# LN, FFN and the output projection of a decode layer: VectorE block transposes in place of selector matmuls, contiguous weight reads, and one load of wo summed in row layout

## The chip, the cores and the metric

The kernel runs on one core of one Trainium2 chip. The metric is device time in microseconds (us), median of several executions. Spans in the traces are shorter than the times (184.9 against 186.1 us in one and the same execution). Each program is traced in one of its executions only, and the stream of loads can lie some tenths of a microsecond earlier or later from one trace to the next (the matmuls that wait for w_up start at 177.45 us in the kernel before, at 177.06 in after_warm); so compare distances within a trace before absolute times. Ratios are computed as the mean time of one kernel's fast runs over that of the other's fast runs of the same rounds, so they are not quite the ratio of the medians quoted beside them.

The engines: PE is TensorE (PEld its weight loads), DVE is VectorE, ACT is ScalarE, POOL is GpSimd, SP issues the DMAs. The granted TensorE clock was not full all the time: "0.50" below is half of full speed, as from 41.79 to 45.20 us in the trace of the kernel before.

## The reference, cut to what matters

One token for each of two batch rows goes through an adaLN-conditioned layer: attention over the last 1024 positions of a cache, then a GEGLU FFN. D = 640, 32 heads of 192, F = 1536, all bf16.

```python
mod = silu(c) @ w_mod                     # six vectors of 640: sa, ca, ga, sb, cb, gb
h = layernorm(x) * (1 + ca) + sa
q = (h @ wq)                              # 640 -> 6144, 32 heads
o = softmax(q k^T / sqrt(192)) v          # for each head, 1024 cached positions
x = x + ga * (o @ wo)                     # 6144 -> 640
h = layernorm(x) * (1 + cb) + sb
x = x + gb * ((gelu(h @ w_gate) * (h @ w_up)) @ w_down)   # 640 -> 1536 -> 640
```

With one token, every weight and cache element is used once or twice: the work is to read 76.88 MB.

## The kernel before

The program has one instruction list for each engine, ordered by semaphores. One SP queue issues all big loads in a fixed order into one arena in SBUF: w_mod, wq, the K and V tiles, wo, w_gate, w_up, w_down. A load waits until the tile whose place it takes has been consumed. The vectors live in "row layout": 640 numbers as 4 groups of 160, group i of batch row b on partition 32*i + 16*b. The kernel's matmuls take them along the partitions instead (h2T in the trace: 128 partitions x 10), so it turns each hidden vector. These are the parts that matter (cut):

```python
WO_SPLIT = [(0, 39), (39, 9)]             # wo in two loads
...
# LN output -> matmul operand: 20 small matmuls with a selector, then a cast out of PSUM
for j in range(KT):
    for i in range(NR):
        e.matmul(ps[32*i:32*i+32, BK_M, CT+2*j:CT+2*j+2], lhsT=hv[:, :, j], rhs=selrow[:, i, :], ...)
S.op("dve", lambda e: e.tensor_copy(out=dst_bf, in_=ps[:, BK_M, CT:CT+2*KT]...))
...
# wo: 4 column groups of TensorE each take every fourth k-tile; two halves of 320 columns
for tl in range(n):
    i = t % NR
    for bk, lo, w in ((2, 0, NA), (3, NA, NA)):
        e.matmul(ps[32*i:32*i+B, bk, 0:w], lhsT=oT[:, t, :], rhs=wv[:, tl, lo:lo+w], ...)
# ... evacuated by ACT and DVE, then summed into row layout by 4 f32 matmuls with selw
...
# gate and up: group i takes columns m*12 + i*3 + r of the weights: runs of 3, 12 apart
wk = wv[:, k, :].rearrange("p (m i r) -> p i m r", i=NR, r=FR)
e.matmul(ps[32*i:32*i+B, bk, 0:FT]..., lhsT=h2T[:, k, :], rhs=wk[:, i, :, :], ...)
...
# FFN activation -> operand of down: 3 matmuls with a selector, then a cast
# down: three loads of w_down (8, 3 and 1 of 12 rows), 48 matmuls of 17 x 160
```

`keep_clock(n)` issues n matmuls on unused data whose only purpose is to keep TensorE busy, so that its clock is not lowered: with 10 of them between gate and up, 8 between up and down and 13 ahead of wo (split_warm below), up ran at a granted clock of 1.00 instead of 0.50 (after_split2).

Of the kernel before, what the change touches and what calls it, by code (L numbers as in the profile page):

```python
# [5 lines left out]
ALU = mybir.AluOpType  # L6
# [113 lines left out]
def bass_adaLN_cond__sliding_block_cached__geglu_ffn__decode_kernel(  # L120
# [29 lines left out]
    FR = 3  # L150
    FC = F // P
    assert B == 2 and D == KT * P and XQ * J == W and XQ * H == P and HB * NR == H and NT * P == NQ
    assert DD * NT == Dh and DD * H == P and NR * FR == FC and FC * P == F and DR == KT * 32 and DD == XQ
# [17 lines left out]
    WO_SPLIT = [(0, 39), (39, 9)]  # L171
# [13 lines left out]
    with es:  # L185
# [18 lines left out]
        place[("wo", 1)] = (13 * HS, wo_n[1])  # L204
        assert 4 * HS + wo_n[0] <= 9 * HS and wo_n[1] <= HS
# [27 lines left out]
        selrow = sb("selrow", [P, NR, B], BF16)  # L233
# [18 lines left out]
        hT = sb("hT", [P, KT, B], BF16)  # L252
        h2T = sb("h2T", [P, KT, B], BF16)
# [7 lines left out]
        oT = sb("oT", [P, NT, B], BF16)  # L261
        selw = sb("selw", [P, RM], F32)
        gl = sb("gl", [P, FT], F32)
        aR = sb("aR", [P, FT], BF16)
        selg = sb("selg", [P, NR, B], BF16)
        aT = sb("aT", [P, FC, RM], BF16)
# [11 lines left out]
        def bank(k):  # L278
            return ("bank", k)
# [67 lines left out]
        for nm, t in (("scT", scT), ("aT", aT)):  # L347
            S.op("pool", lambda e, t=t: e.memset(t[:, :, :], 0.0), writes=[nm], name=nm + "0")
# [8 lines left out]
        S.op("pool", lambda e: e.affine_select(out=selrow[:, :, :], in_=ones_b[:, 0:1].unsqueeze(2).broadcast_to([P, NR, B]),  # L357
                                                pattern=[[-32, NR], [-RB, B]],
                                                compare_op=ALU.is_equal, fill=0.0, base=0, channel_multiplier=1),
             reads=["ones_b"], writes=["selrow"], name="selrow")  # L360
        S.op("pool", lambda e: e.affine_select(out=selg[:, :, :], in_=ones_b[:, 0:1].unsqueeze(2).broadcast_to([P, NR, B]),
                                                pattern=[[-32, NR], [-1, B]],
                                                compare_op=ALU.is_equal, fill=0.0, base=0, channel_multiplier=1),
             reads=["ones_b"], writes=["selg"], name="selg")
        S.op("pool", lambda e: e.memset(selw[:, :], 0.0), writes=["selw"], name="selw0")
        for i in range(NR):
            S.op("pool", lambda e, i=i: e.affine_select(out=selw[:, 0:RM:RB], in_=selw[:, 0:RM:RB], pattern=[[-1, B]],
                                                        compare_op=ALU.not_equal, fill=1.0, base=-32 * i, channel_multiplier=1),
                 reads=["selw"], writes=["selw"], name="selw%d" % (i + 1))
# [66 lines left out]
        def ln_mod(tag, opc_idx, s_idx, dst_bf):  # L436
# [9 lines left out]
            def f(e):  # L446
                last = None
                hv = hrow[:, :].rearrange("p (m j) -> p m j", j=KT)
                for j in range(KT):
                    for i in range(NR):  # L450
                        last = e.matmul(ps[32 * i:32 * i + 32, BK_M, CT + 2 * j:CT + 2 * j + 2], lhsT=hv[:, :, j], rhs=selrow[:, i, :],
                                        start=(j == 0), stop=(j == KT - 1), skip_group_check=True, tile_position=(0, 32 * i))
                return last
            S.op("pe", f, reads=["hrow", "selrow"], writes=[bank(BK_M)], name=tag + "_T")
            S.op("dve", lambda e: e.tensor_copy(out=dst_bf[:, :, :], in_=ps[:, BK_M, CT:CT + 2 * KT].rearrange("p (j b) -> p j b", b=B)),
                 reads=[bank(BK_M)], writes=[tag + "_out"], name=tag + "_out")
# [27 lines left out]
        for w, (k0, nk) in enumerate(WQ_SPLIT):  # L484
            def f(e, w=w, k0=k0, nk=nk):
                last = None
                wv = view(("wq", w)).rearrange("p (k i n) -> p k i n", k=nk, i=NR)
                for kk in range(nk):
                    k = k0 + kk
                    for n in range(NQB):  # L490
                        for i in range(NR):
                            last = e.matmul(ps[32 * i:32 * i + B, n, :], lhsT=hT[:, k, :], rhs=wv[:, kk, i, n * QW:(n + 1) * QW],  # L492
                                            start=(k == 0), stop=(k == KT - 1), tile_position=(0, 32 * i))
# [124 lines left out]
        def p_sel(e):  # L618
            last = None
            for dd in range(DD):  # L620
# [6 lines left out]
        keep_clock(9, "clock0")  # L627

        S.op("act", lambda e: e.activation(out=oT[:, :, :].rearrange("p t b -> p b t"),
                                           in_=ps[:, BK_OT, 0:B * NT].rearrange("p (b t) -> p b t", b=B), func=ACTF.Copy),  # L630
             reads=[bank(BK_OT)], writes=["oT"], name="oT")
        S.op("act", lambda e: e.activation(out=junk[:, :], in_=epsc[:, 0:1], func=ACTF.Sqrt), reads=["epsc"], writes=["junk"], name="sqrt_table")
        S.op("dve", lambda e: e.memset(ps[:, 0:4, :], 0.0), writes=[bank(z) for z in range(4)], name="init_W")
        NA = D // 2
        for ci, (t0, n) in enumerate(WO_SPLIT):
            def f(e, ci=ci, t0=t0, n=n):
                last = None
                wv = view(("wo", ci)).rearrange("p (t n) -> p t n", t=n)
                for tl in range(n):
                    t = t0 + tl  # L640
                    i = t % NR
                    for bk, lo, w in ((2, 0, NA), (3, NA, NA)):
                        last = e.matmul(ps[32 * i:32 * i + B, bk, 0:w], lhsT=oT[:, t, :], rhs=wv[:, tl, lo:lo + w],  # L643
                                        start=(t < NR), stop=(t >= NT - NR), tile_position=(0, 32 * i))
                return last
# [129 lines left out]
```

## Time and profile before

| | before |
|---|---|
| time, median of 3 (range) | 186.01 us (185.92 to 186.16) |
| span of the profiled run | 184.9 us |
| bytes read, mean rate | 76.88 MB, 416 GB/s |
| busy share of the load queue | 96.9% |
| last landing (third part of w_down) | about 182.0 us |

The first lines to read are the page's. The slices cut the span into 40 equal parts; "DMA" is the mean busy share of the 16 DMA engines in tenths, "GB/s" what they moved, and the third line gives a queue's packets, MB and share of the span:

```profile
DMA  9999998999897999999898989899999989899980
GB/s 349 433 495 425 425 425 362 429 425 495 367 511 340 511 404 447 457 394 479 374 479 365 500 351 500 383 468 436 425 450 394 491 367 486 378 388 435 419 365 28
...
q1 hardware_dynamic: 2604, 76.88, 96.9%
```

There is no slice in which the loads stop before the last one. The cause of the alternation of 340 and 511 GB/s was not looked for.

The second view is the timeline of the tail, from the arrival of wo. Columns: start (us), length (us), engine, line, operation, output and inputs, shapes, count, and in brackets the idle time before it and what ended it.

```profile
164.80 2.89 PE L643 MATMUL ps<-arena,oT 128*2 128x320 bf16 x78 [1.78 <-DMA arena<-in_A_wo_dram]
...
168.27 0.98 PE L643 MATMUL ps<-arena,oT 128*2 128x320 bf16 x18 [0.58 <-DMA arena<-in_A_wo_dram]
...
169.28 0.49 DVE L651 COPY arena<-ps 128x320 f32<-128x320 f32 x1 [10.08 <-PE ps L643]
...
169.92 0.47 PE L657 MATMUL ps<-arena,selw 128*17 128x160 f32 x8 [0.67 <-DVE arena L651]
...
170.45 0.33 DVE L664 TENSOR_TENSOR lnt<-ps,modR 128x160 f32<-128x160 f32 x1 [0.67 <-PE ps L657]
...
173.45 0.37 PE L451 MATMUL ps<-selrow,hrow 128*32 128x2 bf16 x20 [0.26 <-DVE hrow L442]
173.87 0.17 DVE L455 CAST h2T<-ps 128x10 bf16<-128x10 f32 x1 [0.48 <-PE ps L451]
...
174.09 1.91 PE L678 MATMUL ps<-arena,h2T 128*2 128x384 bf16 x20 [0.27 <-DVE h2T L455]
...
177.45 1.91 PE L678 MATMUL ps<-arena,h2T 128*2 128x384 bf16 x20 [1.45 <-DMA arena<-in_B_w_up_dram]
...
179.49 0.56 DVE L687 TENSOR_TENSOR aR<-ps,gl 128x384 bf16<-128x384 f32 x1 [5.45 <-PE ps L678]
...
180.38 0.20 DVE L697 CAST aT<-ps 128x24 bf16<-128x24 f32 x1 [0.33 <-PE ps L693]
...
180.65 0.73 PE L706 MATMUL ps<-arena,aT 128*17 128x160 bf16 x32 [0.31 <-DVE aT L697]
...
181.70 0.64 PE L706 MATMUL ps<-arena,aT 128*17 128x160 bf16 x16 [0.31 <-DMA arena<-in_B_w_down_dram]
...
182.39 0.33 DVE L711 TENSOR_TENSOR fin<-ps,modR 128x160 f32<-128x160 f32 x1 [1.81 <-PE ps L706]
```

Read the brackets. The wo matmuls wait for wo twice, up waits 1.45 us for w_up, and the last matmuls wait for w_down. Between those waits there is a chain (evacuation, sums, LN2, gate) that merely has to be finished when the next load lands.

### The profile page before, as it was taken

Reading aid. Unit: us, or ns where it says so; the run is one execution under the profiler, and the core shown is the slowest. Engines: PE = TensorE matmul, PEld = TensorE weight load, DVE = VectorE, ACT = ScalarE, POOL = GpSimd, SP = SyncE. Lnnn points to the kernel's source line nnn. Section 1 sums busy time; section 2 is a strip of 40 time slices with the busy share of each in tenths; the row PEclk is TensorE's granted clock in tenths of the full one; section 3 lists DMA queues with packets and bytes.
Section 4 is the critical chain, followed back from the end, with each engine's and each line's share of the span. In section 5 each row is a group of like instructions: output and inputs, shape, how many; then the busy total and the mean of one; then the engine's idle time right before and its main releaser. Section 6 shows DMA issues by size and latency. Waiting matters only on the chain.

```text
span 184.9 us, 1610 instructions
## 1 busy us (share of the span) xinstructions
PE 104.3 (56%) x843; PEld 26.1 (14%) x552; DVE 106.8 (58%) x97; ACT 14.5 (8%) x28; POOL 6.7 (4%) x29
## 2 busy tenths in 40 slices
PE   0015400937666096662598667748663299866853
PEld 0011000020000000001360002400000266411211
DVE  6213000039996489965994999387995649302311
ACT  2032100060000000001000000100000100220410
POOL 7700000000000000000000000000000000000000
PEclk9999999996999759998599999987999669999999
DMA  9999998999897999999898989899999989899980
GB/s 349 433 495 425 425 425 362 429 425 495 367 511 340 511 404 447 457 394 479 374 479 365 500 351 500 383 468 436 425 450 394 491 367 486 378 388 435 419 365 28
DMA packets 2626, 76.97 MB, mean 416 GB/s; under 512 B 314, under 2 KB 444, under 8 KB 572
## 3 DMA queue, kind: packets, MB, share of 16 engines
q1 hardware_dynamic: 2604, 76.88, 96.9%
q8 instruction: 5, 0.08, 0.2%
q14 instruction: 1, 0.01, 0.0%
q10 hardware_dynamic: 16, 0.01, 0.0%
HBM read 76.88 MB, written 0.00 MB: 416 GB/s over the span
## 4 chain that ended last, share of the span: by engine, by line
DMA 57%; DVE 22%; PE 17%; ACT 1%; issue 1%; SPq 0%
DMA arena<-in_A_k_cache_dram 36%; DMA arena<-in_B_w_down_dram 14%; DVE arena L518 12%; DMA arena<-in_w_mod_dram 8%; PE ps L581 8%; DVE S_sb L537 6%; PE ps L530 5%; DVE Em L567 2%; PE ps L470 2%; DVE negm L547 1%; ACT E_sb L555 1%; PE ps L558 1%; DVE M L543 0%; PE ps L551 0%; SPq L287 0%
## 5 line engine op out<-in xcount | busy, mean ns | idle before, releaser
L530 PE MATMUL ps<-arena,ident_b 128*128 128x512 bf16 x192 | 50.7, 411 | 30.2 <-DVE arena L518 30.1
L518 DVE TENSOR_TENSOR arena<-arena,qbc 128x3072 bf16<-128x3072 bf16 x32 | 54.8, 1749 | 11.1 <-DMA arena<-in_A_k_cache_dram 11.1
L581 PE MATMUL ps<-arena,Em 128*64 128x384 bf16 x256 | 24.5, 357 | 5.6 <-DVE Em L567 5.6
L537 DVE TENSOR_REDUCE S_sb<-ps 128x32 f32<-128x1024 f32 x16 | 19.5, 1219 | 8.4 <-PE ps L530 8.4
L581 PEld LDWEIGHTS ps<-arena,Em 128*64 128x64 bf16 x256 | 15.4, 121 | 29.8 <-DVE Em L567 22.2
L567 DVE TENSOR_TENSOR Em<-E_sb,maskE 128x2048 bf16<-128x2048 bf16 x8 | 18.0, 2282 | 2.6 <-PE ps L581 2.6
L492 PE MATMUL ps<-arena,hT 128*2 128x512 bf16 x60 | 4.7, 485 | 11.7 <-DMA arena<-in_A_wq_dram 11.7
L502 DVE CAST qrow<-ps 128x512 bf16<-128x512 f32 x1 | 0.7, 693 | 15.6 <-PE ps L492 15.6
L545 PEld LDWEIGHTS ps<-ident_f,M 128*1 128x1 f32 x2 | 0.2, 80 | 61.5 <-DVE M L543 61.5
L555 ACT ACTIVATE E_sb<-S_sb,nbias 128x256 bf16<-128x256 f32 x2 | 1.0, 507 | 69.3 <-DVE nbias L553 69.3
L651 DVE COPY arena<-ps 128x320 f32<-128x320 f32 x1 | 0.5, 491 | 10.1 <-PE ps L643 10.1
L643 PE MATMUL ps<-arena,oT 128*2 128x320 bf16 x96 | 3.9, 299 | 2.4 <-DMA arena<-in_A_wo_dram 2.4
L588 ACT ACTIVATE On<-ps,rden 128x384 bf16<-128x384 f32 x2 | 1.2, 582 | 47.5 <-PE ps L581 47.5
L403 PE MATMUL ps<-ident_b,crow 2*128 2x2 bf16 x5 | 0.4, 177 | 7.9 <-POOL zsel L383 7.9
L678 PE MATMUL ps<-arena,h2T 128*2 128x384 bf16 x40 | 3.8, 455 | 1.7 <-DMA arena<-in_B_w_up_dram 1.4
L470 PE MATMUL ps<-arena,scT 128*17 128x480 bf16 x40 | 4.3, 597 | 0.5 <-DMA arena<-in_w_mod_dram 0.5
L415 PE MATMUL ps<-Em,ident_b 128*128 128x512 bf16 x17 | 4.2, 379 | 0.2 <-issue 0.2
L408 DVE CAST X<-xr 128x160 f32<-128x160 bf16 x1 | 0.2, 244 | 6.1 <-DMA xr<-in_A_x_dram 6.1
L687 DVE TENSOR_TENSOR aR<-ps,gl 128x384 bf16<-128x384 f32 x1 | 0.6, 558 | 5.4 <-PE ps L678 5.4
L424 PE MATMUL ps<-st,selstat 128*128 128x2 f32 x4 | 0.9, 298 | 4.9 <-ACT sqj L420 4.9
L478 DVE TENSOR_SCALAR opc<-modR 128x160 f32<-128x160 f32 x2 | 0.5, 245 | 5.1 <-ACT modR L475 5.1
L492 PEld LDWEIGHTS ps<-arena,hT 128*2 128x2 bf16 x20 | 0.6, 100 | 15.8 <-issue 15.8
(89 smaller groups left out, 52.6 us busy)
## 6 DMA issues: line engine op xcount, KB each, us to landing
arena<-in_A_v_cache_dram SPq DMA_DIRECT2D x4, 6144.0 KB, 27.2
arena<-in_A_k_cache_dram SPq DMA_DIRECT2D x3, 6144.0 KB, 36.0
arena<-in_A_wq_dram SPq DMA_DIRECT2D x1, 7680.0 KB, 31.3
arena<-in_A_wo_dram SPq DMA_DIRECT2D x1, 6240.0 KB, 27.0
arena<-in_A_k_cache_dram SPq DMA_DIRECT2D x2, 3072.0 KB, 42.7
arena<-in_w_mod_dram SPq DMA_DIRECT2D x1, 4800.0 KB, 14.0
arena<-in_B_w_gate_dram SPq DMA_DIRECT2D x1, 1920.0 KB, 20.7
arena<-in_B_w_up_dram SPq DMA_DIRECT2D x1, 1920.0 KB, 22.7
```

The costliest lines, as they stand in the source:

```text
L415: last = e.matmul(ps[:, BK_T, :], lhsT=ident_b[:, :], rhs=Em[:, 0, 0:512 // H, :].rearrange("p j h -> p (j h)"), start=True, stop=True)
L470: last = e.matmul(ps[32 * i:32 * i + RM, half, 0:MH].rearrange("p (m n) -> p m n", n=DR), lhsT=scT[:, k, :], rhs=wv[:, 3 * half:3 * half + ...
L492: last = e.matmul(ps[32 * i:32 * i + B, n, :], lhsT=hT[:, k, :], rhs=wv[:, kk, i, n * QW:(n + 1) * QW], start=(k == 0), stop=(k == KT - 1) ...
L518: S.op("dve", lambda e: e.tensor_tensor(out=kt, in0=kt, in1=qbc[:, b, :].unsqueeze(1).broadcast_to([P, JC, Dh]), op=ALU.mult), reads=[("qb ...
L530: last = e.matmul(o_ap, lhsT=ident_b[:, :], rhs=kt[:, :, t * GC:(t + 1) * GC], start=(t == 0), stop=(t == NCH - 1))
L537: S.op("dve", lambda e: e.tensor_reduce(out=S_sb[:, b, 2 * JC * pair:2 * JC * (pair + 1)], in_=ps[:, 2 * z:2 * z + 2, :].rearrange("p k (j ...
L547: S.op("dve", lambda e: e.tensor_reduce(out=negm[:, b, :].rearrange("p (h x) -> p h x", x=XQ), in_=ps[0:1, BK_T, 0:P].rearrange("p (h x) - ...
L555: S.op("act", lambda e: e.activation(out=E_sb[:, b, :], in_=S_sb[:, b, :], func=ACTF.Exp, scale=SCALE, bias=nbias[:, b:b + 1], accum_out=d ...
L567: S.op("dve", lambda e, z=z, j=j: e.tensor_tensor(out=Em[:, z, :, :], in0=E_sb[:, b, j:j + JE].unsqueeze(2).broadcast_to([P, JE, H]), in1= ...
L581: last = e.matmul(ps[64 * i:64 * i + 2 * H, BK_O, 0:ON], lhsT=Em[:, z, 2 * jp:2 * jp + 2, :].rearrange("p j h -> p (j h)"), rhs=view(it, l ...
L643: last = e.matmul(ps[32 * i:32 * i + B, bk, 0:w], lhsT=oT[:, t, :], rhs=wv[:, tl, lo:lo + w], start=(t < NR), stop=(t >= NT - NR), tile_po ...
L678: last = e.matmul(ps[32 * i:32 * i + B, bk, 0:FT].rearrange("p (m r) -> p m r", r=FR), lhsT=h2T[:, k, :], rhs=wk[:, i, :, :], start=(k == ...
```

## The change

The intent: take the selector matmuls and PSUM casts out of the chain by letting VectorE transpose blocks in SBUF (one instruction: 0.35 us for 128 x 160, and the result is correct); since the transpose of the FFN activation reads columns 12 apart by itself (0.85 us for 128 x 384), let gate and up read their weights contiguously; and sum wo directly in row layout, which removes the evacuation and the summing matmuls, at the price of 192 matmuls of 160 columns instead of 96 of 320, all behind one load.

```diff
-    WO_SPLIT = [(0, 39), (39, 9)]
+    WO_SPLIT = [(0, NT)]
...
-            S.op("pe", f, ..., name=tag + "_T")          # 20 selector matmuls
-            S.op("dve", lambda e: e.tensor_copy(out=dst_bf..., in_=ps[...]), ...)
+            S.op("dve", lambda e: e.transpose(dst_bf[:, :, :], hrow[:, :].rearrange("p (m j) -> p j m", j=KT)), ...)
...
-        keep_clock(9, "clock0")
+        keep_clock(24, "clock0")
...
-        # 96 matmuls of 320 columns, ACT and DVE evacuation, 4 summing matmuls
+            for t in range(NT):
+                for i in range(NR):
+                    last = e.matmul(ps[32 * i:32 * i + RM, 2, 0:DR], lhsT=oT[:, t, :], rhs=wv[:, t, i, :],
+                                    start=(t == 0), stop=(t == NT - 1), tile_position=(0, 32 * i))
...
-                        wk = wv[:, k, :].rearrange("p (m i r) -> p i m r", i=NR, r=FR)
-                            last = e.matmul(..., lhsT=h2T[:, k, :], rhs=wk[:, i, :, :], ...)
+                            last = e.matmul(..., lhsT=h2T[:, k, 0:RM], rhs=wv[:, k, i * FT:(i + 1) * FT], ...)
...
-        S.op("pe", a_T, reads=["aR", "selg"], writes=[bank(2)], name="aT_T")
-        S.op("dve", lambda e: e.tensor_copy(out=aT..., in_=ps[:, 2, 0:FC * B]...), ...)
+        S.op("dve", lambda e: e.transpose(aT[:, :, :], aR[:, :].rearrange("p (m r) -> p r m", r=FC)), ...)
```

Left out: the POOL setup of the removed selectors, buffer shapes, the operand view of q, and that the gelu result is kept in the place of an earlier buffer (`S_sb`).

More of the change, by code (lines that the diff above doesn't have):

```diff
@@ L149, in bass_adaLN_cond__sliding_block_cached__geglu_ffn__decode_kernel @@
     DD = Dh // NT
-    FR = 3
     FC = F // P
     assert B == 2 and D == KT * P and XQ * J == W and XQ * H == P and HB * NR == H and NT * P == NQ
-    assert DD * NT == Dh and DD * H == P and NR * FR == FC and FC * P == F and DR == KT * 32 and DD == XQ
+    assert DD * NT == Dh and DD * H == P and FC * P == F and DR == KT * 32 and DD == XQ
     SCALE = float(Dh) ** -0.5
@@ L203, in bass_adaLN_cond__sliding_block_cached__geglu_ffn__decode_kernel @@
         place[("wo", 0)] = (4 * HS, wo_n[0])
-        place[("wo", 1)] = (13 * HS, wo_n[1])
-        assert 4 * HS + wo_n[0] <= 9 * HS and wo_n[1] <= HS
+        assert wo_n[0] == 5 * HS
         o_g = 9 * HS
@@ L232, in bass_adaLN_cond__sliding_block_cached__geglu_ffn__decode_kernel @@
         selstat = sb("selstat", [P, P], F32)
-        selrow = sb("selrow", [P, NR, B], BF16)
         selq = sb("selq", [P, B, HB * SQW], BF16)
@@ L251, in bass_adaLN_cond__sliding_block_cached__geglu_ffn__decode_kernel @@
         hrow = sb("hrow", [P, DR], BF16)
-        hT = sb("hT", [P, KT, B], BF16)
-        h2T = sb("h2T", [P, KT, B], BF16)
+        hT = sb("hT", [P, KT, 32], BF16)
+        h2T = sb("h2T", [P, KT, 32], BF16)
         S_sb = sb("S_sb", [P, B, J], F32)
@@ L260, in bass_adaLN_cond__sliding_block_cached__geglu_ffn__decode_kernel @@
         On = sb("On", [P, B, ON], BF16)
-        oT = sb("oT", [P, NT, B], BF16)
-        selw = sb("selw", [P, RM], F32)
-        gl = sb("gl", [P, FT], F32)
+        oT = sb("oT", [P, NT, RM], BF16)
+        assert FT <= B * J
+        gl = S_sb[:, :, :].rearrange("p b j -> p (b j)")[:, 0:FT]
         aR = sb("aR", [P, FT], BF16)
-        selg = sb("selg", [P, NR, B], BF16)
-        aT = sb("aT", [P, FC, RM], BF16)
+        aT = sb("aT", [P, FC, 32], BF16)
         fin = sb("fin", [P, DR], F32)
@@ L346, in bass_adaLN_cond__sliding_block_cached__geglu_ffn__decode_kernel @@
         S.op("pool", lambda e: e.memset(epsc[:, 1:2], EPS), reads=["epsc"], writes=["epsc"], name="epsc1")
-        for nm, t in (("scT", scT), ("aT", aT)):
+        for nm, t in (("scT", scT), ("oT", oT)):
             S.op("pool", lambda e, t=t: e.memset(t[:, :, :], 0.0), writes=[nm], name=nm + "0")
@@ L356, in bass_adaLN_cond__sliding_block_cached__geglu_ffn__decode_kernel @@
              reads=["ident_f"], writes=["ident_b"], name="ident_b")
-        S.op("pool", lambda e: e.affine_select(out=selrow[:, :, :], in_=ones_b[:, 0:1].unsqueeze(2).broadcast_to([P, NR, B]),
-                                                pattern=[[-32, NR], [-RB, B]],
-                                                compare_op=ALU.is_equal, fill=0.0, base=0, channel_multiplier=1),
-             reads=["ones_b"], writes=["selrow"], name="selrow")
-        S.op("pool", lambda e: e.affine_select(out=selg[:, :, :], in_=ones_b[:, 0:1].unsqueeze(2).broadcast_to([P, NR, B]),
-                                                pattern=[[-32, NR], [-1, B]],
-                                                compare_op=ALU.is_equal, fill=0.0, base=0, channel_multiplier=1),
-             reads=["ones_b"], writes=["selg"], name="selg")
-        S.op("pool", lambda e: e.memset(selw[:, :], 0.0), writes=["selw"], name="selw0")
-        for i in range(NR):
-            S.op("pool", lambda e, i=i: e.affine_select(out=selw[:, 0:RM:RB], in_=selw[:, 0:RM:RB], pattern=[[-1, B]],
-                                                        compare_op=ALU.not_equal, fill=1.0, base=-32 * i, channel_multiplier=1),
-                 reads=["selw"], writes=["selw"], name="selw%d" % (i + 1))
         S.op("pool", lambda e: e.memset(selq[:, :, :], 0.0), writes=["selq"], name="selq0")
@@ L444, in ln_mod @@
                  reads=["lnt", "rstd", ("modR", s_idx // 3)], writes=["hrow"], name=tag + "_h")
-            def f(e):
-                last = None
-                hv = hrow[:, :].rearrange("p (m j) -> p m j", j=KT)
-                for j in range(KT):
-                    for i in range(NR):
-                        last = e.matmul(ps[32 * i:32 * i + 32, BK_M, CT + 2 * j:CT + 2 * j + 2], lhsT=hv[:, :, j], rhs=selrow[:, i, :],
-                                        start=(j == 0), stop=(j == KT - 1), skip_group_check=True, tile_position=(0, 32 * i))
-                return last
-            S.op("pe", f, reads=["hrow", "selrow"], writes=[bank(BK_M)], name=tag + "_T")
-            S.op("dve", lambda e: e.tensor_copy(out=dst_bf[:, :, :], in_=ps[:, BK_M, CT:CT + 2 * KT].rearrange("p (j b) -> p j b", b=B)),
-                 reads=[bank(BK_M)], writes=[tag + "_out"], name=tag + "_out")
+            S.op("dve", lambda e: e.transpose(dst_bf[:, :, :], hrow[:, :].rearrange("p (m j) -> p j m", j=KT)),
+                 reads=["hrow"], writes=[tag + "_out"], name=tag + "_T")
         ln_stats("ln1")
@@ L491, in f @@
                         for i in range(NR):
-                            last = e.matmul(ps[32 * i:32 * i + B, n, :], lhsT=hT[:, k, :], rhs=wv[:, kk, i, n * QW:(n + 1) * QW],
+                            last = e.matmul(ps[32 * i:32 * i + B, n, :], lhsT=hT[:, k, 0:RM:RB], rhs=wv[:, kk, i, n * QW:(n + 1) * QW],
                                             start=(k == 0), stop=(k == KT - 1), tile_position=(0, 32 * i))
@@ L626, in bass_adaLN_cond__sliding_block_cached__geglu_ffn__decode_kernel @@
         S.op("pe", p_sel, reads=[("On", b) for b in range(B)] + ["zsel"], writes=[bank(BK_OT)], name="sel")
-        keep_clock(9, "clock0")
-        S.op("act", lambda e: e.activation(out=oT[:, :, :].rearrange("p t b -> p b t"),
+        keep_clock(24, "clock0")
+        S.op("act", lambda e: e.activation(out=oT[:, :, 0:RM:RB].rearrange("p t b -> p b t"),
                                            in_=ps[:, BK_OT, 0:B * NT].rearrange("p (b t) -> p b t", b=B), func=ACTF.Copy),
-             reads=[bank(BK_OT)], writes=["oT"], name="oT")
+             reads=[bank(BK_OT), "oT"], writes=["oT"], name="oT")
@@ L632, in bass_adaLN_cond__sliding_block_cached__geglu_ffn__decode_kernel @@
         S.op("act", lambda e: e.activation(out=junk[:, :], in_=epsc[:, 0:1], func=ACTF.Sqrt), reads=["epsc"], writes=["junk"], name="sqrt_table")
         S.op("dve", lambda e: e.memset(ps[:, 0:4, :], 0.0), writes=[bank(z) for z in range(4)], name="init_W")
-        NA = D // 2
-        for ci, (t0, n) in enumerate(WO_SPLIT):
-            def f(e, ci=ci, t0=t0, n=n):
-                last = None
-                wv = view(("wo", ci)).rearrange("p (t n) -> p t n", t=n)
-                for tl in range(n):
-                    t = t0 + tl
-                    i = t % NR
-                    for bk, lo, w in ((2, 0, NA), (3, NA, NA)):
-                        last = e.matmul(ps[32 * i:32 * i + B, bk, 0:w], lhsT=oT[:, t, :], rhs=wv[:, tl, lo:lo + w],
-                                        start=(t < NR), stop=(t >= NT - NR), tile_position=(0, 32 * i))
-                return last
-            S.op("pe", f, reads=keys(("wo", ci)) + ["oT"], writes=[bank(2), bank(3)], name="wo%d" % ci)
@@ L647, in bass_adaLN_cond__sliding_block_cached__geglu_ffn__decode_kernel, with wo_f @@
-        wo_sum = ("v", 1, 1)
-        wS = view(wo_sum, 0, 2 * D).bitcast(F32)
-        S.op("act", lambda e: e.activation(out=wS[:, 0:NA], in_=ps[:, 2, 0:NA], func=ACTF.Copy),
-             reads=[bank(2)], writes=keys(wo_sum, 0, 2 * NA), name="wo_evac0")
-        S.op("dve", lambda e: e.tensor_copy(out=wS[:, NA:D], in_=ps[:, 3, 0:NA]),
-             reads=[bank(3)], writes=keys(wo_sum, 2 * NA, 2 * NA), name="wo_evac1")
-        def wo_rows(e):
-            last = None
-            for i in range(NR):
-                last = e.matmul(ps[32 * i:32 * i + RM, BK_M, 0:DR], lhsT=selw[:, :], rhs=wS[:, i * DR:(i + 1) * DR],
-                                start=True, stop=True, tile_position=(0, 32 * i))
+        def wo_f(e):
+            last = None
+            wv = view(("wo", 0)).rearrange("p (t i n) -> p t i n", t=NT, i=NR)
+            for t in range(NT):
+                for i in range(NR):
+                    last = e.matmul(ps[32 * i:32 * i + RM, 2, 0:DR], lhsT=oT[:, t, :], rhs=wv[:, t, i, :],
+                                    start=(t == 0), stop=(t == NT - 1), tile_position=(0, 32 * i))
@@ L659, in wo_rows @@
             return last
-        S.op("pe", wo_rows, reads=keys(wo_sum, 0, 2 * D) + ["selw"], writes=[bank(BK_M)], name="wo_rows")
+        S.op("pe", wo_f, reads=keys(("wo", 0)) + ["oT"], writes=[bank(2)], name="wo")
         keep_clock(5, "clock1")
         assert queue["next"] == len(items)
-        S.op("dve", lambda e: e.tensor_tensor(out=lnt[:, :], in0=ps[:, BK_M, 0:DR], in1=modR[:, 2, :], op=ALU.mult),
-             reads=[bank(BK_M), ("modR", 0)], writes=["lnt"], name="ga_attn")
+        S.op("dve", lambda e: e.tensor_tensor(out=lnt[:, :], in0=ps[:, 2, 0:DR], in1=modR[:, 2, :], op=ALU.mult),
+             reads=[bank(2), ("modR", 0)], writes=["lnt"], name="ga_attn")
@@ L675, in f @@
                     for k in range(k0, k0 + nk):
-                        wk = wv[:, k, :].rearrange("p (m i r) -> p i m r", i=NR, r=FR)
                         for i in range(NR):
-                            last = e.matmul(ps[32 * i:32 * i + B, bk, 0:FT].rearrange("p (m r) -> p m r", r=FR), lhsT=h2T[:, k, :],
-                                            rhs=wk[:, i, :, :], start=(k == 0), stop=(k == KT - 1), tile_position=(0, 32 * i))
+                            last = e.matmul(ps[32 * i:32 * i + RM, bk, 0:FT], lhsT=h2T[:, k, 0:RM], rhs=wv[:, k, i * FT:(i + 1) * FT],
+                                            start=(k == 0), stop=(k == KT - 1), tile_position=(0, 32 * i))
                     return last
@@ L686, in bass_adaLN_cond__sliding_block_cached__geglu_ffn__decode_kernel @@
         ffn_gu(1, wu_v, "up", [(k0, nk, ("wu", ci)) for ci, (k0, nk) in enumerate(WU_SPLIT)])
-        S.op("dve", lambda e: e.tensor_tensor(out=aR[:, :], in0=ps[:, 1, 0:FT], in1=gl[:, :], op=ALU.mult),
+        S.op("dve", lambda e: e.tensor_tensor(out=aR[:, :], in0=ps[:, 1, 0:FT],
+                                              in1=gl[:, :], op=ALU.mult),
              reads=[bank(1), "gl"], writes=["aR"], name="geglu")
-        def a_T(e):
-            last = None
-            for r in range(FR):
-                last = e.matmul(ps[:, 2, NR * B * r:NR * B * (r + 1)], lhsT=aR[:, :].rearrange("p (m r) -> p m r", r=FR)[:, :, r],
-                                rhs=selg[:, :, :].rearrange("p i b -> p (i b)"), start=True, stop=True)
-            return last
-        S.op("pe", a_T, reads=["aR", "selg"], writes=[bank(2)], name="aT_T")
-        S.op("dve", lambda e: e.tensor_copy(out=aT[:, :, 0:RM:RB].rearrange("p (i r) b -> p i r b", r=FR),
-                                            in_=ps[:, 2, 0:FC * B].rearrange("p (r i b) -> p i r b", r=FR, i=NR)),
-             reads=[bank(2)], writes=["aT"], name="aT")
+        S.op("dve", lambda e: e.transpose(aT[:, :, :], aR[:, :].rearrange("p (m r) -> p r m", r=FC)), reads=["aR"], writes=["aT"], name="aT")
         for ci, (r0, nr) in enumerate(WD_SPLIT):
@@ L705, in f @@
                     for i in range(NR):
-                        last = e.matmul(ps[32 * i:32 * i + RM, BK_OT, CY:CY + DR], lhsT=aT[:, fc, :], rhs=wv[:, i, :],
+                        last = e.matmul(ps[32 * i:32 * i + RM, BK_OT, CY:CY + DR], lhsT=aT[:, fc, 0:RM], rhs=wv[:, i, :],
                                         start=(fc == WD_SPLIT[0][0]), stop=(fc == WD_SPLIT[-1][0]), tile_position=(0, 32 * i))
```

## The prediction

> **What bounds the kernel now.** The stream of loads. On the page, the queue that carries nearly all bytes is busy 96.9% of the span: 76.88 MB, 416 GB/s. Cut into stretches, DMA moves 390 to 470 GB/s from 4 to 179 us without a pause. Every load of the stream is issued 14 to 46 us before it lands (the DMA view), so a buffer freed a few us sooner or later delays no byte. The chain of waits ends in the load of w_down.
>
> In the tail (timeline, from 160 us) the loads set the pace: the two parts of wo land at about 164.7 and 168.2 us, w_up at 177.4, the three of w_down at about 180.5, 181.65 and 182.0. The last matmuls, two VectorE operations and the store follow; the span ends at 184.9.
>
> **What changes, costed.**
> - LN1: 20 small matmuls and a cast (18.09 to 18.68 us) become a block transpose. The q projection waits 11.7 us for wq anyway: worth nothing.
> - wo: 78 of 96 matmuls ran before the second part landed; from that landing (168.2) to the next operation (170.45) passed 2.25 us: matmuls 0.98, evacuation 0.49, row sums 0.47. Now 192 matmuls of 160 columns start after one load, which has the same bytes and should land at 168.2. The w_down matmuls (same shape) follow each other every 16 ns ((0.73 - 0.23)/31), so 192 take 3.1 + 0.25 us; the next operation starts at about 171.7, 1.2 us LATER. The 24 clock-keeping matmuls (236 ns each) end by 166.8 and delay nothing.
> - LN2: from hrow to h2T took 0.65 us. [...] h2T comes at about 175.1 instead of 174.0.
> - Gate and up: 20 matmuls take 1.91 us each, 1.0 column per ns and column group; the wo matmuls reach 2.2. Weights were read in runs of 3 elements, 12 apart, and now contiguously. [...] I expect 1.0 to 1.1 us each. Gate ends near 176.2; up still waits for w_up at 177.4 and ends at about 178.5 instead of 179.4.
> - geglu unchanged (0.56 us). Its transpose reads 384 columns with a stride: [...] against 0.53 for matmuls and cast. aT ready at about 179.8 instead of 180.6.
> - down: waits for w_down as before.
> - POOL loses about 2 us of setup, before the first load lands at 14.0: nothing.
>
> **On the critical path: nothing.** The stream keeps its bytes (one DMA fewer of 17), and the operations after the last landing stay. Predicted 185.9 us, 8 in 10 between 185.3 and 186.6; faster by over 2% 0.01, within 2% 0.97, slower by over 2% 0.02.
>
> **What would show it.** The wo matmuls start at about 168.2 and span about 3.4 us; LN2 starts about 1.2 us later; gate and up about 1.0 us each; [...] the last wait is still on w_down, at about 182; DMA share and GB/s as before.
>
> **What would make it wrong.** wo matmuls at half clock or bound by 192 weight loads (over 5.5 us), a strided transpose over 1.5 us: beyond 2 us together they push aT past 181 us, and the end follows one for one. Or the stream running at another rate, by a per cent, with wo in one piece.

What the sum came to: the next operation after wo at 171.7 us, h2T at 175.1, gate ended at 176.2 and up at 178.5, aT at 179.8, and 185.9 us for the whole. The step from 171.7 to 175.1 and the one from 178.5 to 179.8 each contain a transpose. The 1.0 to 1.1 us for gate and for up is an estimate: 1.91 us were measured at 1.0 column per ns, and the 2.2 columns per ns of the wo matmuls would give 0.87 us.

## The result, and the profile after

| | before | after |
|---|---|---|
| time, median of 6 (range) | 185.97 us (185.90 to 186.16) | 185.95 us (185.82 to 186.21) |
| ratio (95% interval) | | 1.000 (0.9987 to 1.0013) |
| span of the profiled run | 184.9 us | 184.8 us |

All runs are fast ones. The time is the same. The page's lines for the stream, after:

```profile
DMA  9999998999898999999998989899999999989980
GB/s 341 441 482 439 426 426 356 426 426 504 367 500 351 500 404 458 458 394 458 395 479 376 479 372 479 383 479 447 415 447 404 495 429 439 426 343 406 423 362 35
...
q1 hardware_dynamic: 2460, 76.88, 96.9%
```

The bytes and the queue's share are those of before. The timeline of the tail, after:

```profile
168.32 5.14 PE L614 MATMUL ps<-arena,oT 128*17 128x160 bf16 x192 [2.51 <-DMA arena<-in_A_wo_dram]
...
173.52 0.32 DVE L621 TENSOR_TENSOR lnt<-ps,modR 128x160 f32<-128x160 f32 x1 [14.75 <-PE ps L614]
...
176.51 0.35 DVE L429 STREAM_TRANSPOSE h2T<-hrow 128x160 bf16<-128x160 bf16 x1
...
176.92 1.80 PE L634 MATMUL ps<-arena,h2T 128*17 128x384 bf16 x40 [0.65 <-DVE h2T L429]
...
178.84 0.56 DVE L643 TENSOR_TENSOR aR<-ps,S_sb 128x384 bf16<-128x384 f32 x1 [1.98 <-PE ps L634]
179.44 0.85 DVE L646 STREAM_TRANSPOSE aT<-aR 128x384 bf16<-128x384 bf16 x1
...
180.54 0.73 PE L653 MATMUL ps<-arena,aT 128*17 128x160 bf16 x32 [1.82 <-DMA arena<-in_B_w_down_dram]
181.61 0.66 PE L653 MATMUL ps<-arena,aT 128*17 128x160 bf16 x16 [0.34 <-DMA arena<-in_B_w_down_dram]
...
182.32 0.32 DVE L658 TENSOR_TENSOR fin<-ps,modR 128x160 f32<-128x160 f32 x1 [2.04 <-PE ps L653]
```

Three things moved, and they cancel before the end is reached. The operation after wo starts 3.07 us later (173.52 against 170.45). Gate and up then take 1.80 us together, without a wait, where they had taken 1.91 us each with a wait between. At 180.54 down starts where it had started at 180.65, and it now waits for w_down there: the new chain is ready at 180.29 (179.44 + 0.85).

Why did 192 matmuls take 5.14 us? Busy time of that line in half-microsecond stretches; the columns are the stretch, its length, busy PE, busy PEld, granted clock, DMA share, GB/s:

```profile
168.00:168.50 0.50, 0.17 (x12) 0.18 (x16) 1.00 1.08 461
168.50:169.00 0.50, 0.50 (x28) 0.50 (x22) 0.57 0.86 369
...
171.50:172.00 0.50, 0.50 (x28) 0.50 (x20) 0.52 1.15 492
172.00:172.50 0.50, 0.50 (x40) 0.50 (x32) 1.00 1.01 430
```

At a clock of 0.50 some 24 to 28 matmuls start in half a microsecond, at 1.00 it is 40. The clock stood at half for about 3.4 us. TensorE had idled 2.51 us before, in spite of the 24 clock matmuls.

The gap alone is not the cause. wo_only and after_stride below have the same 24 clock matmuls, gaps of 2.25 and 2.17 us before wo, and a granted clock of 1.00 in it. The traces show a grid: in those of the two kernels, all changes of the granted clock (eleven in each) lie whole multiples of 3.413 us apart, to within 0.02 us (here 21.79, ..., 168.57, 171.98, 182.22 us, read off stretches of 0.1 us), and the grid lies elsewhere in each of the two. In nine of the twelve runs below, tables of stretches show a change of clock in the tail, and stretches of this length can be counted from there. From 160 us on, in these eleven traces, a full-clock stretch of this grid in which TensorE was busy for 0.19 to 0.41 of the time was followed by one at half clock, and one with 0.50 or more by another at full clock. (Earlier in the traces the division is less clean: in the kernel before, three stretches without any matmul, from 21.3 to 31.6 us, were each followed by full clock.) Here TensorE was busy 0.90 us of the stretch from 165.16 to 168.57, a share of 0.26; in wo_only 1.83 us (0.54) and in after_stride 1.69 us (0.50) of the stretch before wo. So whether these wo matmuls meet a half clock depends on where the grid falls in a run. How many of the six timed runs met it is not known; one trace was kept.

### The profile page after: what moved, and what is told of

Its sections match the earlier page's. It is cut to its first block, busy times and chain, and to the rows that moved or that the text cites. A ratio compares the mean times of both kernels' runs of the same rounds, so it can differ in the third digit from the quotient of the medians.

```text
span 184.8 us, 1749 instructions
## 1 busy us (share of the span) xinstructions
PE 104.7 (57%) x905; PEld 29.6 (16%) x645; DVE 106.0 (57%) x96; ACT 14.4 (8%) x27; POOL 6.0 (3%) x22
## 4 chain that ended last, share of the span: by engine, by line
DMA 58%; DVE 24%; PE 15%; ACT 1%; issue 1%; SPq 0%
DMA arena<-in_A_k_cache_dram 36%; DMA arena<-in_B_w_down_dram 14%; DVE arena L492 14%; PE ps L555 8%; DMA arena<-in_w_mod_dram 8%; DVE S_sb L511 6%; PE ps L504 3%; DVE Em L541 2%; PE ps L444 2%; DVE negm L521 1%; ACT E_sb L529 1%; PE ps L532 1%; PE ps L525 1%; DVE M L517 0%; SPq L283 0%
## 5 line engine op out<-in xcount | busy, mean ns | idle before, releaser
L504 PE MATMUL ps<-arena,ident_b 128*128 128x512 bf16 x192 | 48.6, 393 | 30.3 <-DVE arena L492 30.2
L555 PE MATMUL ps<-arena,Em 128*64 128x384 bf16 x256 | 25.5, 367 | 5.6 <-DVE Em L541 5.6
L555 PEld LDWEIGHTS ps<-arena,Em 128*64 128x64 bf16 x256 | 15.9, 124 | 30.3 <-DVE Em L541 22.2
L398 PE MATMUL ps<-Em,ident_b 128*128 128x512 bf16 x34 | 7.8, 379 | 0.0
L614 PE MATMUL ps<-arena,oT 128*17 128x160 bf16 x192 | 5.1, 290 | 2.5 <-DMA arena<-in_A_wo_dram 2.5
L614 PEld LDWEIGHTS ps<-arena,oT 128*17 128x17 bf16 x192 | 4.9, 117 | 7.8 <-DMA arena<-in_A_wo_dram 7.8
L653 PE MATMUL ps<-arena,aT 128*17 128x160 bf16 x48 | 1.4, 234 | 2.2 <-DMA arena<-in_B_w_down_dram 2.2
L519 PE MATMUL ps<-ident_f,M 128*1 128x128 f32 x2 | 0.5, 270 | 3.5 <-DVE M L517 3.5
## 6 DMA issues: line engine op xcount, KB each, us to landing
arena<-in_A_wq_dram SPq DMA_DIRECT2D x1, 7680.0 KB, 31.6
```

The lines of the kernel that those rows point to most:

```text
L398: last = e.matmul(ps[:, BK_T, :], lhsT=ident_b[:, :], rhs=Em[:, 0, 0:512 // H, :].rearrange("p j h -> p (j h)"), start=True, stop=True)
L504: last = e.matmul(o_ap, lhsT=ident_b[:, :], rhs=kt[:, :, t * GC:(t + 1) * GC], start=(t == 0), stop=(t == NCH - 1))
L555: last = e.matmul(ps[64 * i:64 * i + 2 * H, BK_O, 0:ON], lhsT=Em[:, z, 2 * jp:2 * jp + 2, :].rearrange("p j h -> p (j h)"), rhs=view(it, l ...
L614: last = e.matmul(ps[32 * i:32 * i + RM, 2, 0:DR], lhsT=oT[:, t, :], rhs=wv[:, t, i, :], start=(t == 0), stop=(t == NT - 1), tile_position ...
```

## The experiments

The theory: the load stream sets the end, and in both kernels the tail of compute runs with a slack behind it, so neither part of the change is worth anything, nor do they have to balance. The main rival: wo costs 3 us and LN and FFN give 3 us back, and the equal time is a cancellation on the path. A second rival: the single load of wo changed the stream itself.

### wo_only: only the wo part

```diff
 (the kernel before)
-    WO_SPLIT = [(0, 39), (39, 9)]
+    WO_SPLIT = [(0, NT)]
+    (192 matmuls in row layout, 24 clock matmuls; LN, gate, up and aT as before)
```

> The kernel before with only the wo part of the change (one load, 192 matmuls in row layout, 24 clock matmuls); LN and FFN as before. Theory (the load stream sets the end; the tail has a slack of about 0.6 us at the down matmuls in the kernel before): LN2 starts about 3 us later if the wo matmuls run at half clock for 3.4 us as in the profiled run of after, the slow gate and up (1.91 us each) then end near 181.0, aT comes near 182.1 and the end slips by about 0.9 us (0.5%); with a full clock in the wo matmuls, 0 us. Rival (both parts lie fully on the path and cancel): +3 us (1.6%).

Measured: 185.93 us (185.83 to 186.33, 4 runs), before 185.95; ratio 1.0001 (0.9986 to 1.0016). Lines of its timeline:

```profile
168.00 3.50 PE L639 MATMUL ps<-arena,oT 128*17 128x160 bf16 x192 [2.25 <-DMA arena<-in_A_wo_dram]
...
175.21 4.04 PE L660 MATMUL ps<-arena,h2T 128*2 128x384 bf16 x40 [0.28 <-DVE h2T L454]
...
180.53 0.73 PE L688 MATMUL ps<-arena,aT 128*17 128x160 bf16 x32 [0.30 <-DVE aT L679]
```

Here the wo matmuls ran at a granted clock of 1.00 and took 3.50 us, after an idle time of 2.25 us. So the next operation came 1.1 us later (171.56 against 170.45). The wait for w_up of 1.45 us took that up: down starts at 180.53, as before. The cancelling rival asked for +3 us and is out, for this clock state. What half the clock would have done here was not seen in the profile; one of the four runs took 186.33 us, and no trace of it was kept. before_delay below puts 3.48 us into the same place and loses 1.27 us.

### ffn_only: only the LN and FFN part

```diff
 (the kernel after)
-    WO_SPLIT = [(0, NT)]
+    WO_SPLIT = [(0, 39), (39, 9)]
+    (wo matmuls, evacuation, summing matmuls and 9 clock matmuls as before)
```

> The kernel before with only the LN and FFN part (block transposes, contiguous gate and up); wo as before. Theory: gate and up take about 0.9 us each in place of 1.9, up still waits for w_up at 177.4, aT is ready about 0.7 us sooner and waits for w_down; the time is the same as before within 0.1 us. Rival (both parts on the path and cancelling): 2 to 3 us faster (1.1 to 1.6%).

Measured: 186.27 us (186.15 to 186.47, 4 runs), before 185.95; ratio 1.0019 (1.0002 to 1.0035). Lines of its timeline:

```profile
173.55 0.99 PE L658 MATMUL ps<-arena,h2T 128*17 128x384 bf16 x20 [0.65 <-DVE h2T L436]
...
177.20 1.78 PE L658 MATMUL ps<-arena,h2T 128*17 128x384 bf16 x20 [2.66 <-DMA arena<-in_B_w_up_dram]
...
180.60 1.78 PE L677 MATMUL ps<-arena,aT 128*17 128x160 bf16 x48 [1.61 <-DVE aT L670]
```

The rival's gain of 2 to 3 us is not there. But the result is not the same either: 0.3 us slower. Gate took 0.99 us, up 1.78 us with the same instructions. Because gate was done so early, TensorE idled for 2.66 us before w_up landed (it was busy for 0.99 of the 3.41 us from 173.53), and the granted clock was then 0.50 from 177 us to the end. Slow up and slow down together make the harm: aT is ready only at 180.54, and 48 matmuls at half clock from 180.60 last until 182.38, 5.18 us after up started at the landing of w_up; in the kernel before this is 4.89 us (182.34 - 177.45). A chain that is faster ahead of a load ended later behind it.

### after_split: the changed kernel with wo in two loads

```diff
-    WO_SPLIT = [(0, NT)]
+    WO_SPLIT = [(0, 39), (39, 9)]
+    (row-layout matmuls, 156 behind the first load and 36 behind the second)
```

> The changed kernel with wo loaded in two parts again (39 and 9 of 48), matmuls still in row layout. Theory: 156 of the 192 matmuls run before the second part lands at 168.2, the next operation starts near 169.2 instead of 173.5, four us earlier, and the time is the same within 0.1 us because the end waits for w_down. Rival (the one load of wo changed the rate of the stream, or the tail of compute sets the time): a time off by over 0.2 us.

Measured: 186.18 us (186.16 to 186.22, 4 runs), before 185.95; ratio 1.0011 (0.9996 to 1.0026). Run again with five rounds beside the last experiments, as after_split2:

> The same kernel as after_split, run beside the other two to compare on one chip: about 186.2 again.

Measured: 186.25 us (186.11 to 186.34, 5 runs), before 185.96; ratio 1.0014 (1.0001 to 1.0026). The first of these in the timeline:

```profile
177.27 1.78 PE L637 MATMUL ps<-arena,h2T 128*17 128x384 bf16 x20 [2.51 <-DMA arena<-in_B_w_up_dram]
...
180.66 1.78 PE L656 MATMUL ps<-arena,aT 128*17 128x160 bf16 x48 [1.62 <-DVE aT L649]
```

And two stretches of it (length, busy PE, PEld, DVE, ACT, POOL, then granted clock, DMA share, GB/s):

```profile
177.00:178.00 1.00, 0.73 (x12) 0.39 (x16) 0.00 (x0) 0.00 (x0) 0.00 (x0) 0.50 0.98 410
...
180.40:182.40 2.00, 1.74 (x48) 1.45 (x48) 0.21 (x1) 0.00 (x0) 0.00 (x0) 0.50 0.17 65
```

The next operation after wo started at 170.37 in the first run, 3.15 us before that of the changed kernel (expected was 169.2; the 24 clock matmuls held wo back until 166.8), and the time did not fall. It rose by 0.2 us. That could be the second load or the clock; the pattern of a half clock in up and down is that of ffn_only. split_delay and split_warm below separate the two.

### after_warm: 34 clock matmuls ahead of wo

```diff
-        keep_clock(24, "clock0")
+        keep_clock(34, "clock0")
```

> The changed kernel with 34 instead of 24 clock matmuls ahead of wo, so TensorE is busy until about 168.0. Theory: the 192 wo matmuls took 5.14 us because the clock was granted at 0.50 for 3.4 us of them; kept busy they run at full clock and take 3.3 to 3.5 us; the time is the same within 0.1 us. Rival (192 weight loads bind): still about 5 us at a full granted clock.

Measured: 185.82 us (185.69 to 185.94, 4 runs), before 185.95; ratio 0.9991 (0.9976 to 1.0006). Lines of its timeline:

```profile
168.84 3.50 PE L614 MATMUL ps<-arena,oT 128*17 128x160 bf16 x192
...
180.28 1.78 PE L653 MATMUL ps<-arena,aT 128*17 128x160 bf16 x48 [2.23 <-DMA arena<-in_B_w_down_dram]
```

The wo matmuls ran at a granted clock of 1.00 and took 3.50 us. So the clock was the cause of the 5.14 us, not the number of weight loads: 192 of them were issued here too. Because the clock matmuls held wo back until 168.84, the next operation came 1.13 us sooner (172.39 against 173.52), not the full 1.64; that shortened the kernel by nothing that stands clear of noise. TensorE now idled for 2.23 us between up and down, and down ran at 0.50, all 48 matmuls in 1.78 us; but it began at 180.28, when the first part of w_down landed, and so ended at 182.06, where the kernel before ended down at 182.34: half the clock in down alone did no harm.

### before_delay, warm_delay, split_delay: measuring the slack

```diff
+        for z in range(3):                    # 0.91 us each, zeros into two free PSUM banks
+            S.op("dve", lambda e: e.memset(ps[:, 0:2, :], 0.0), reads=["lnt"], writes=[bank(0), bank(1)], ...)
         S.op("dve", lambda e: e.tensor_tensor(out=X[:, :], in0=lnt[:, :], in1=X[:, :], op=ALU.add), ...)
-        keep_clock(5, "clock1")
+        keep_clock(17, "clock1")
```

The same edit in three kernels: the one before, after_warm, and after_split.

> The kernel before with about 2.8 us of VectorE memsets (3 of 0.91 us) in the chain between wo and LN2, and 12 more clock matmuls so that TensorE does not cool meanwhile. It measures the slack. Theory: gate starts 2.8 us later (176.9), up no longer waits for w_up, aT comes near 181.8 instead of 180.6, and the end slips by 0.5 to 0.7 us, not 2.8. Rival (the tail of compute is the path): +2.8 us.

> The changed kernel with warm wo matmuls and the same delay. Theory: gate from about 178.6, gate and up 1.8 us together, transpose 0.85 us, aT near 182.1; the end slips by 0.9 to 1.2 us: once exposed, the changed tail is some tenths LONGER than the one before, although its matmuls are faster, because the single wo load puts 3.4 us of matmuls after the landing. Rival: +2.8 us; or less than before_delay, if the changed tail is the shorter one.

> The changed kernel with wo in two parts and the same delay. Theory: gate from about 176.6, up still at the landing of w_up (177.3), so the delay costs nothing beside after_split (0 +- 0.15 us), unless the clock state of the last matmuls differs. Rival: +2.8 us.

In before_delay the granted clock was 1.00 throughout, from 168 to 185 us. The memsets were 0.29 us apart, so the delay was larger than planned. In before_delay the add behind them started at 174.31 instead of 170.81, that is 3.84 us after the multiplication instead of 0.36: the delay is 3.48 us. Measured:

| | time (runs) | before, same rounds | ratio (95% interval) |
|---|---|---|---|
| before_delay | 187.20 us (186.92 to 187.31) | 185.93 | 1.0065 (1.005 to 1.008) |
| warm_delay (one run of four slow) | 187.22 us of all, 186.71 us of the fast (186.55 to 189.69) | 185.93 | 1.0064 (1.0026 to 1.0102) |
| split_delay | 185.97 us (185.88 to 186.02) | 185.93 | 1.000 (0.9986 to 1.0015) |

Two lines of the timeline of before_delay, gate with up and the start of down:

```profile
177.58 3.68 PE L680 MATMUL ps<-arena,h2T 128*2 128x384 bf16 x40 [0.27 <-DVE h2T L455]
...
182.53 1.01 PE L708 MATMUL ps<-arena,aT 128*17 128x160 bf16 x48 [0.29 <-DVE aT L699]
```

The same of warm_delay:

```profile
178.50 1.81 PE L636 MATMUL ps<-arena,h2T 128*17 128x384 bf16 x40 [0.65 <-DVE h2T L429]
...
181.93 1.01 PE L655 MATMUL ps<-arena,aT 128*17 128x160 bf16 x48 [1.62 <-DVE aT L648]
```

The same of split_delay:

```profile
176.21 2.04 PE L639 MATMUL ps<-arena,h2T 128*17 128x384 bf16 x40 [0.65 <-DVE h2T L430]
...
180.46 0.73 PE L658 MATMUL ps<-arena,aT 128*17 128x160 bf16 x32 [2.20 <-DMA arena<-in_B_w_down_dram]
```

Of 3.48 us put into the chain of the kernel before, 1.27 us reached the end (187.20 - 185.93). The other 2.2 us is its slack from LN2 on. With the delay neither up nor down waits for a load in before_delay: the chain is bare from LN2 on. In warm_delay it is bare too, and there down starts 0.60 us sooner. So the expectation that the bare changed tail would be some tenths longer was wrong in the profiled run: gate and up save more (1.81 against 3.68 us) than the wo landing costs. The timed runs do not settle it: the fast ones were 186.55, 186.71 and 187.74 us, and a fourth, 189.69, counts as slow; what the spread is was not found.

split_delay hid all of the delay. It was also faster than after_split, which has 3.48 us less to do: 185.88 to 186.02 against 186.16 to 186.22 and 186.11 to 186.34 us. With the delay, gate ends just as w_up lands, TensorE does not idle there, and up runs at a clock of 1.00. (From 181.3 us on this run too has a clock of 0.50; its last 16 down matmuls take 0.71 us, those of split_warm below 0.65.) The second load of wo is in both kernels, so it is not what made after_split slower.

### after_stride: what the strides cost (wrong result)

```diff
-  rhs=wv[:, k, i * FT:(i + 1) * FT]
+  rhs=wv[:, k, :].rearrange("p (m i r) -> p i m r", i=NR, r=3)[:, i, :, :]
-  e.transpose(aT[:, :, :], aR[:, :].rearrange("p (m r) -> p r m", r=FC))
+  e.transpose(aT[:, :, :], aR[:, :].rearrange("p (r m) -> p r m", r=FC))
   (and the same for the LN transposes: contiguous)
```

> Wrong result on purpose: the changed kernel with gate and up reading the weights in runs of 3 elements, 12 apart, as before, and with both transposes reading contiguously. Theory: gate and up go back from 0.9 to 1.9 us each at full granted clock (the stride is the cost, not the 2 or 17 columns of the stationary operand); the transposes keep 0.35 and 0.85 us, because they took 2.2 ns for each column in both strides, so the stride costs VectorE nothing. Rival: transposes of 0.2 and 0.45 us (about one column per ns) when contiguous; or gate and up still near 0.9 us.

Measured, a single run: 185.95 us, before 185.93. Lines of its timeline:

```profile
174.56 0.35 DVE L429 STREAM_TRANSPOSE h2T<-hrow 128x160 bf16<-128x160 bf16 x1
174.96 1.90 PE L634 MATMUL ps<-arena,h2T 128*17 128x384 bf16 x20 [0.64 <-DVE h2T L429]
...
179.83 0.58 DVE L646 STREAM_TRANSPOSE aT<-aR 128x384 bf16<-128x384 bf16 x1
```

Gate is back at 1.90 us with 17 columns of stationary operand, at a granted clock of 1.00: the stride is the cost on TensorE, as expected. On VectorE the expectation failed in half: reading with a step of 5 elements (10 bytes) costs nothing measurable (0.354 us strided, 0.346 contiguous), but a step of 12 elements (24 bytes) costs 0.27 us (0.848 against 0.578). On TensorE the runs of 3, 12 apart, take 1.9 times as long as contiguous columns (1.90 us here against 0.99 in ffn_only). Why a step of 5 costs VectorE nothing and one of 12 does was not tested.

### split_warm and after_warm2: is there a version that beats both?

```diff
 (split_warm: after_split, with clock matmuls in every wait of the tail)
-        keep_clock(24, "clock0")
+        keep_clock(13, "clock0")
+        keep_clock(10, "clock3")         # between gate and up
+        keep_clock(8, "clock4")          # between up and down
 (after_warm2: after_warm, with the last two only, 1 and 8)
```

> The changed kernel with wo in two parts, and clock matmuls in every wait of TensorE in the tail: 13 ahead of wo, 10 between gate and up, 8 between up and down. Theory: after_split and ffn_only were 0.1 to 0.2% slower because TensorE idled for 2.5 us before up and then ran up and down at a granted clock of 0.50 (48 down matmuls in 1.78 us instead of about 1.4); kept busy, the clock stays at 1.00 and the time comes down by 0.15 to 0.3 us against after_split, to 185.8 to 186.0, at or just below the kernel before. Rival (the second wo load costs the time): stays near 186.2.

> after_warm (one wo load, 34 clock matmuls) with 8 more between up and down, where after_warm's down ran at 0.50 clock (1.78 us). Theory: down at full clock ends at the landing of the last part of w_down plus 0.65 us; 0 to 0.2 us faster than after_warm's 185.8. If it beats the kernel before at all, it is by 0.1 to 0.2%.

Measured in the rounds of after_split2: split_warm 185.90 us (185.84 to 186.01, 5 runs), ratio 0.9998 (0.9985 to 1.0012); after_warm2 186.02 us (185.73 to 186.37, 5 runs), ratio 1.0005 (0.9992 to 1.0018). The timeline of split_warm:

```profile
177.16 0.99 PE L637 MATMUL ps<-arena,h2T 128*17 128x384 bf16 x20 [1.24 <-DMA arena<-in_B_w_up_dram]
...
180.35 0.73 PE L658 MATMUL ps<-arena,aT 128*17 128x160 bf16 x32 [0.37 <-DMA arena<-in_B_w_down_dram]
181.41 0.65 PE L658 MATMUL ps<-arena,aT 128*17 128x160 bf16 x16 [0.33 <-DMA arena<-in_B_w_down_dram]
```

All of split_warm's runs lie below all of after_split2's on the same chip, with wo in two loads in both. The edit is clock matmuls alone, and up takes 0.99 us again. From the start of up to the first operation after down it is 5.23 us in ffn_only, after_split and after_split2, 4.94 in the kernel before and 4.96 in split_warm; so the 0.3 us came from the clock in the idle tail. But nothing beats the kernel before: the last matmuls still wait for w_down. after_warm2's expected gain is there only in the run that was traced, its fastest (185.73 us, down at full clock); two of its runs, at 186.33 and 186.37 us, stay unexplained. Where the clock grid fell in them is one candidate; no trace of them was kept.

### split_short: a shorter stream (wrong result)

```diff
 (split_warm with 1 and 6 clock matmuls between gate, up and down)
-        place[("wg", 0)] = (o_g, KT * F)
-        ffn_gu(0, wg_v, "gate", [(0, KT, ("wg", 0))])
+        ffn_gu(0, wu_v, "gate", [(0, KT, ("wu", 0))])
```

> Wrong result on purpose: split_warm without the load of w_gate (gate reads w_up's tile; 1 clock matmul between gate and up, 6 between up and down), so the stream is 1.97 MB shorter, 4.6 us at the 425 GB/s of the tail, and nothing else ends sooner. Theory (the stream sets the end and the changed tail, with wo in two parts, has several us of slack): w_up lands near 172.7, w_down near 175.9, 177.0 and 177.3, the last wait is still on w_down and the time falls by 4.3 to 4.7 us (2.4%). Rival (compute of the tail is as long as the stream, so the change just balances on the path): it falls by less than 2 us.

Measured: 181.43 us (181.30 to 181.74, 4 runs), before 185.97; ratio 0.9759 (0.9743 to 0.9775). Lines of its timeline:

```profile
172.81 0.99 PE L636 MATMUL ps<-arena,h2T 128*17 128x384 bf16 x20 [1.08 <-DMA arena<-in_B_w_up_dram]
...
176.67 1.01 PE L657 MATMUL ps<-arena,aT 128*17 128x160 bf16 x48 [0.22 <-DVE aT L649]
```

Taking 1.97 MB out of the stream takes 4.5 us off the time, and the matmuls that wait for w_up start 4.35 us sooner than in split_warm (172.81 against 177.16). This is the direct evidence that the stream sets the end; three microseconds of compute taken out of the chain (after_split) or put in again (split_delay) had moved the end by 0.2 to 0.3 us, and in the wrong direction. One detail differs from what was expected: down waits for aT and no longer for w_down. At this length of the stream, compute and loads are about even, even in the version with the shortest tail.

## Why the prediction was right

**The whole.** 185.9 us was predicted (185.3 to 186.6), 185.95 measured, "within 2%" as forecast. The reason given, that nothing of the change lies on the critical path because the stream of loads sets the end, is borne out by split_short (the time follows the stream), by before_delay (2.2 us of slack) and by wo_only and after_warm (a shift of more than a microsecond in the chain leaves the end where it was).

**The step that was mis-sized: wo.** The prediction had the 192 wo matmuls take 3.4 us and the next operation start at 171.7, "1.2 us LATER". In the profiled run they took 5.14 us and it started at 173.52, 3.07 us later. The rate was right for a full clock: 3.50 us in wo_only and after_warm. The clock was wrong: the prediction only asked whether the 24 clock matmuls would delay wo, and counted on a full clock after them; they ended at 165.8, and the stretch of the clock grid before wo was busy for 0.26 of its length. It named half clock as a risk, but put its size at "over 5.5 us". The end did not move because the next operation had slack to use up; that the number held in spite of this miss is the slack's doing, which the prediction had argued for but not measured.

**LN transposes.** 0.354 us measured for h2T. An estimate for other widths, a line through the two contiguous transposes of after_stride (0.346 us for 160 columns, 0.578 for 384): 1.04 ns a column and 0.18 us on top.

**Gate and up.** Predicted 1.0 to 1.1 us each; measured 0.99 (ffn_only), and 1.80 for both back to back. That the runs of 3 had been the cost was right (after_stride: 1.90 us with them, at a granted clock of 1.00). That up would wait for w_up was right for a full clock, and not in the profiled run, where wo was so late that gate ended after w_up had landed.

**The aT transpose.** Measured 0.85 us, 0.27 of it for the stride (after_stride). aT was ready at 180.29 instead of 179.8, still ahead of w_down.

**What the prediction did not see.** It looked for danger only in a chain that gets longer. The runs show danger in one that gets shorter: with gate done early, TensorE idles (2.66 us in ffn_only, 2.51 in after_split, 2.07 in after_split2), the granted clock is 0.50 from there to the end, and the matmuls behind the last landing are slower (ffn_only +0.19%, after_split +0.11 and +0.14%). In the profiled run the change avoids this because its wo part is late enough to leave no gap before up; the prediction did not count on that, so this much was luck. That it holds in every run is argued, not shown.

**What stays open.** The spread of after_warm2 and warm_delay; and the end of the stream itself: between 179 and 182 us the loads move far less than before (265, 134 and 50 GB/s in the three microseconds of the changed kernel's profile) while w_down is still being waited for. No run tried to change that; time may be left there.

## What to carry to other kernels

When one stream of loads sets the time, read the tail as a row of appointments: each chain only has to be ready when its load lands, and making it faster moved nothing here (after_warm: 1.13 us sooner after wo, ratio 0.9991). Measure the slack by putting a known delay into the chain, and the bound by taking known bytes out of the stream. And look at what a faster chain does to the engine that then waits: here a TensorE left idle for about 2.5 us of a 3.4 us stretch had half its clock in the next, just where the last matmuls had to run, so a few fill matmuls in the wait, not fewer instructions, were what kept the time.

## What the runs measured of the hardware

- The granted clock. Gaps of TensorE of 2.51 us (wo in the changed kernel, up in after_split), 2.66 us (up in ffn_only), 2.07 us (up in after_split2) and 2.23 us (down in after_warm) were followed by a clock of 0.50, one of 2.25 us (wo in wo_only) was not: the length alone does not decide. In the traces of the two kernels all changes of the clock lie on a grid of 3.413 us, and the half clock in wo lasted from 168.57 to 171.98. From 160 us on, in the eleven traces that could be counted, full-clock stretches of this length in which TensorE was busy for 0.19 to 0.41 of the time were followed by half a clock in the next.
- Matmuls in different column groups. The 192 wo matmuls of 160 columns, spread over four column groups, took 3.50 us at a granted clock of 1.00 (wo_only), and one matmul of this shape lasts 0.23 us; so (3.50 - 0.23)/191 = 17 ns from start to start, on average.
- Strided reads of bf16. TensorE reading its moving operand in runs of 3, 12 apart: 1.90 us (after_stride) against 0.99 us (ffn_only) for 20 matmuls of 384 columns. A VectorE transpose of 384 columns with a step of 12: 0.848 us against 0.578; of 160 columns with a step of 5: 0.354 against 0.346.
